# A Fourier-mixing and gated feed-forward kernel: a new order of start-up, weight conversions through PSUM, and the first chunk's outputs in row tiles

## The chip, the cores and the metric

The kernel runs on one core of one Trainium2 chip. Its time is that of one execution on the device in microseconds; the number for a kernel is the median of several executions. One further execution was recorded by the hardware profiler, and every row of the profile comes from that one. TensorE is called PE in the rows (PEld is its weight load), VectorE DVE, ScalarE ACT, GpSimd POOL, and SP is the engine that issues most transfers.

## The reference

The input x has 8 sequences of 3008 rows of 256 numbers. The real part of a two-dimensional Fourier transform of each sequence goes through a gated feed-forward layer of width 1536. Only x is float32; the three weights arrive as float64.

```
X = np.fft.fft(x, axis=1)
X = np.fft.fft(X, axis=2)
h = X.real.astype(np.float32).reshape(8 * 3008, 256)
gate = 1.0 / (1.0 + np.exp(-(h @ w_gate)))
val = h @ w_val
out = (gate * val @ w_out).astype(np.float32)
```

## The kernel before

**The mathematics as tiled.** The transform over the 256 features is a 256x256 cosine/sine matrix (`dt`), and it is multiplied into `w_gate` and `w_val` once, at the start (`merge`, line 329): each of the 2x6 pieces of 256 columns costs four matmuls and gives a piece of `G1` (the cosine half) and `G2` (the sine half). The transform over the 3008 rows is a matmul of folded x against a table of cosines and sines (`ST`, from `stab`): for each sequence it gives two arrays, `pk` and `qk` (`PQE[b][0]` and `PQE[b][1]`), of 128 x 1505. One feature, the middle one of 256, stands apart: its row over the frequencies is `ek`, and its part in the layer is the product of `ek` with a column `ge` taken from the first row of `G2`. The rows and their mirror images share this work: one front tile gives both, as a sum and a difference.

**The loops.** A sequence has 6 chunks of at most 252 frequencies (`chunks`), a chunk 12 tiles of 128 of the 1536 hidden units (`NFT`), so the main loop (line 915 on) has 576 iterations `i`. An iteration does, in program order on each engine:

- `seed` (593), from the second chunk on: ACT writes `ek` times `ge` into a PSUM bank `PF[i]`, once for gate and once for value; `front_a` (602) adds two matmuls with `pk`. In the first chunk there is no seed. For i < 5 (`N1`) two more matmuls, of `G2` with a tile that is zero but for one row of `ek`, do its work; from 5 to 11 DVE does it in `part` (line 619).
- `part` (611) copies twice the bank to SBUF (`ae`); `front_b` (623) adds two matmuls with `qk`. Now the bank holds one of the two row sets, and `ae` minus the bank the other.
- `gate_a` and `gate_b` (628, 647), for tile i-1: sigmoid on ACT, difference and two products on DVE; they give `h`. After the second and third of three tiles POOL forms 13 sums and differences of thirds of `h` (`H_SUMS`, line 660), which the next step needs.
- `back` (667), for the group of three tiles whose first is i-5, i-6 or i-7: a bilinear scheme that multiplies 3x3 blocks of `h` by 3x2 blocks of `w_out` in 15 matmuls of 168 columns, five to an iteration, into five PSUM banks (`po`). It needs sums of `w_out` blocks (`wf`, made by `forms`, 342; POOL makes the first of four groups, DVE the other three). After four groups ACT and DVE copy the banks to `c`, and `finish` (739) sums and transposes them on DVE, a few operations per iteration (`later`), and stores rows. The last group of the program goes another way (`rows_out`, 705): plain `h` as the stationary operand, `w_out` with 256 columns as the moving one.

PSUM has eight banks: five `po` and three that `bank()` hands out in turn.

**The weights.** A piece of 256x256 float64 values is loaded as integers and becomes float32 on three engines: two ACT operations (`weight_parts`, lines 297 and 298), three DVE operations in place in SBUF (`weight_join`, 307, 308, 310), one POOL addition (312). `jobs` gives the order of the 18 pieces, with gate, value and output pieces mixed; the first ten have homes in buffers that are free at the start, the rest use the buffer of x.

**The order of the start (lines 800 to 853)**, which is written out by hand as every engine's order is. SP issues: two weight pieces, x of sequence 0 in two halves, the cosine table in two halves, three pieces, half the sine table, two pieces, the other half, three pieces. The first two pieces are converted and merged; their `ge` columns go from `G2` to `ge` by small transfers on the ACT queue (later ones on SP). x is folded in two halves (`fold_ops(0, 3)`, DVE and a part on POOL), PE makes `pk` and `ek` (the latter with one column of x repeated 128 times as the stationary operand, so that all 128 rows get it), then `qk`. Between the copies of these results six more pieces are converted. Merges 3 to 12 are spread over iterations -1 to 8 (`use`), conversions too (`pre`). Further steps that the change moves: x of sequence 1 is loaded at iteration 14 (`load_x(1)`), and the row of `ek` for the next chunk is fetched eight iterations ahead (`e_rows`).

The helpers `e_load`, `e_fold` and `e_sums` (531 to 567) make the `ek` rows of sequences 1 to 7 later, with seven rows at once and four results at partitions 0, 32, 64 and 96 of one bank.

Of the kernel before, what the change touches and what calls it, by code (L numbers as in the profile page):

```python
# [82 lines left out]
def kernel(  # L83
# [61 lines left out]
    def load_x(b):  # L145
        X[b] = xp.tile([P, 4, NQ, D], F32, name="x4", tag="x4")
        for h in range(0, 4, 2):
            if b:
                nc.sync.dma_start(out=X[b][:, h : h + 2], in_=XR[b][:, h : h + 2])
            else:  # L150
                nc.sync.dma_start(out=X[b][0:NP, h : h + 2], in_=xf[b, :, h : h + 2])
# [29 lines left out]
    G1 = const.tile([P, 2, F], F32, name="G1")  # L181
    G2 = const.tile([P, 2, F], F32, name="G2")
# [9 lines left out]
    def load_table(t, nq):  # L192
        for q in range(0, NQ, nq):
            yield nc.sync.dma_start(out=ST[0][0:NP, t, q : q + nq], in_=stab[:, t, q : q + nq])
# [14 lines left out]
    def table_odd():  # L209
# [21 lines left out]
        def tangent():  # L231
# [12 lines left out]
    KEEP = 10  # L244

    def weight_load(j):
# [13 lines left out]
        def home(j):  # L260

            if j in (0, 1, 2, 3, 5):
                if j > 2:
                    ws = some(5, pqp, "qk")[:, (j // 5) * 2 * WC : (j // 5 + 1) * 2 * WC]
                    return sp.tile([P, 4 * WC], F32, name="raw", tag="sf"), ws
                t = hp.tile([P, 6 * WC], F32, name="raw", tag="h")
                return t[:, 0 : 4 * WC], t[:, 4 * WC :]
            if j in (4, 6, 9):
                t = wf[:, {4: 1, 6: 2, 9: 3}[j]].rearrange("p m n -> p (m n)")
                return t[:, 0 : 4 * WC], t[:, 4 * WC : 6 * WC]  # L270
            t = some(10, cp, "c")
            if j == 7:
                raw = pqp.tile([P, 4 * WC], F32, name="raw", tag="pk")
                return raw, t[:, 6 * WC : 8 * WC]
            return t[:, 0 : 4 * WC], t[:, 4 * WC : 6 * WC]
# [3 lines left out]
        else:  # L279
            both = some(24, xp, "x4").rearrange("p (i n) -> p i n", n=2 * WC)  # L280
            r, i = (j - KEEP) % 3 * 2, 6 + (j - KEEP) % 6
            raw, ws = both[:, r : r + 2].rearrange("p a n -> p (a n)"), both[:, i]
# [17 lines left out]
    def weight_join(j):  # L300
# [4 lines left out]
        wi = ws.bitcast(I32)  # L305
        ts = nc.vector.tensor_scalar
        ts(out=ws, in0=ws, scalar1=2.0 ** -15, scalar2=HUGE, op0=ALU.max, op1=ALU.min)
        ts(out=wi, in0=wi, scalar1=3, scalar2=0x3FFFFFF8, op0=ALU.logical_shift_left,
           op1=ALU.bitwise_and)
        nc.vector.scalar_tensor_tensor(out=wi, in0=hi, scalar=-(2 ** 30), in1=wi,  # L310
# [17 lines left out]

    def merge(ws, g, c, other):
        cs = slice(c * WC, (c + 1) * WC)  # L330
        ps = bank("ps", other)
# [4 lines left out]
        nc.scalar.copy(G2[:, g, cs], ps[:, WC : 2 * WC])  # L336
        nc.scalar.copy(G1[:, g, cs], ps[:, 0:WC])
        for f in range(c * WC // P, (c + 1) * WC // P):
            (nc.sync if c else nc.scalar).dma_start(
                out=ge[:, g, f : f + 1], in_=G2[0:1, g, f * P : (f + 1) * P])  # L340

    def forms(g):
# [4 lines left out]
        engine = nc.vector if g else nc.gpsimd  # L347
# [38 lines left out]
    def fold_ops(b, nq):  # L386
# [51 lines left out]
        else:  # L438

            def half1(q):  # L440
                point(nc.vector, 2, 3, q)
                first(nc.vector, 2, 3, q)
                for blk in range(2):
                    across(nc.vector, blk, q)
                    feat(nc.vector, *parts[blk], q)

            def half2(q):
                across(nc.vector, 0, q)
                feat(nc.vector, *parts[0], q)
                across(pool, 1, q)  # L450
# [545 lines left out]
```

## Time and profile before

| what | value |
|---|---|
| median of 3 runs | 1947.07 us (1945.73 to 1947.19) |
| the profiled execution | 1951.1 us, of which the span of its instructions is 1949.0 us |
| mean granted TensorE clock | 0.997 |
| DMA traffic | 97.85 MB |

The span is counted from the first to the last instruction on the core; the 2.1 us that the execution takes beyond it lie around it. In a timeline row stand the start and the duration in us, the engine, the line, the operation, its output and inputs, the number of instructions, and in brackets the idle time before and what ended it. Two records of PE belong to one float32 matmul of the program, so `x4` of `pf` rows is two matmuls. Matmuls are pipelined: the pace of a series is the difference of the starts of two rows, not the duration of one. In rows of groups stand count, total busy us, mean ns, and idle time before them with its causes. Rows of windows give the busy time and number of instructions per engine in a stretch, then the granted clock, the share of time that the DMA engines were busy, and GB/s.

### The profile page before, as it was taken

The page shows a single profiled execution, that of the slowest core. Times are in us where ns is not written, and L with a number is a line of the kernel's source. Part 1 is how long each engine was busy: PE and PEld are TensorE (multiplying, and loading weights), DVE is VectorE, ACT ScalarE, POOL GpSimd, SP SyncE. Part 2 cuts the span into 40 slices and gives each one's busy share as a digit, 9 for nine tenths or more (in the row PEclk, how much of TensorE's full clock was granted, in tenths as well). Part 3 has the DMA queues.
Part 4 walks back from the last instruction along what each step waited for, and adds up shares of the span by engine and source line. Part 5 has one row for each costly group of instructions (what it writes and reads, how often), then busy time and mean ns, then how long its engine had stood idle before and what let it go on. Part 6 is the DMA issues. An engine that isn't in the chain of part 4 may idle for free.

```text
span 1949.0 us, 34556 instructions
## 1 busy us (share of the span) xinstructions
PE 1917.7 (98%) x11262; PEld 1789.8 (92%) x11262; DVE 1461.0 (75%) x3269; ACT 1332.5 (68%) x3125; POOL 1589.7 (82%) x2842
## 2 busy tenths in 40 slices
PE   6999999999999999999999999999999999999999
PEld 3789889999999999999999999999999999999998
DVE  6777787787777777777777777777777777776776
ACT  3567757776777677776777767777677776777775
POOL 3779998997889878987889878888788886777775
PEclk8999999999999999999999999999999999999999
DMA  8352513212012120222012021221210110011101
GB/s 270 90 145 20 118 32 111 47 25 82 14 47 58 17 79 14 57 49 79 14 25 78 18 79 23 45 53 20 82 20 14 19 23 14 14 20 22 25 16 31
DMA packets 168565, 97.85 MB, mean 50 GB/s; under 512 B 131803, under 2 KB 160070, under 8 KB 165838
## 3 DMA queue, kind: packets, MB, share of 16 engines
q1 hardware_dynamic: 167254, 95.12, 20.5%
q8 instruction: 91, 1.49, 0.3%
q14 instruction: 88, 0.72, 0.1%
q10 hardware_dynamic: 1100, 0.51, 0.1%
q0 software_dynamic: 32, 0.00, 0.0%
HBM read 70.35 MB, written 47.24 MB: 60 GB/s over the span
## 4 chain that ended last, share of the span: by engine, by line
PE 92%; DVE 4%; DMA 2%; ACT 1%; issue 0%; SPq 0%; ACTq 0%; DVEq 0%
PE pf L135 48%; PE po L135 40%; PE ev L135 3%; DMA st<-in_stab_dram 1%; DVE c L754 1%; PE od L135 1%; DMA ge<-G 1%; PE ps L135 1%; DVE z L640 1%; ACT pf L653 0%; DVE h L654 0%; DVE h L652 0%; PE row L135 0%; DVE wf L375 0%; DMA raw<-in_moe_w_val_dram 0%
## 5 line engine op out<-in xcount | busy, mean ns | idle before, releaser
L660 POOL TENSOR_TENSOR sf<-h 128x168 f32<-128x168 f32 (+1 forms) x955 | 530.8, 574 | 225.1 <-DVE h L654 225.0
L660 POOL TENSOR_TENSOR sf<-h,sf 128x168 f32<-128x168 f32 (+1 forms) x1146 | 638.4, 576 | 61.5 <-DVE h L654 60.9
L135 PE MATMUL pf<-qk,G 128*128 128x252 f32 (+1 forms) x2304 | 583.2, 376 | 4.2 <-DVE ae L619 2.3
L135 PE MATMUL pf<-pk,G 128*128 128x252 f32 (+1 forms) x2304 | 583.5, 376 | 1.6 <-DVE h L654 1.4
L654 DVE TENSOR_TENSOR h<-pf,z 128x252 f32<-128x252 f32 (+1 forms) x576 | 241.5, 419 | 420.0 <-ACT pf L653 420.0
L600 ACT ACTIVATE pf<-ek,ge 128x252 f32<-128x252 f32 (+1 forms) x1128 | 531.4, 471 | 18.7 <-DVE h L654 0.2
L135 PE MATMUL po<-sf,wf 128*128 128x168 f32 (+1 forms) x3056 | 527.5, 305 | 0.0
L616 ACT ACTIVATE ae<-pf 128x504 f32<-128x504 f32 (+1 forms) x569 | 335.0, 589 | 233.8 <-PE pf L135 232.5
L135 PEld LDWEIGHTS pf<-pk,G 128*128 128x128 f32 x2304 | 436.1, 190 | 55.7 <-DVE h L654 3.2
L135 PEld LDWEIGHTS po<-sf,wf 128*128 128x128 f32 x3056 | 470.4, 190 | 8.2
L135 PE MATMUL po<-h,wf 128*128 128x168 f32 (+1 forms) x2674 | 473.9, 306 | 0.2 <-DVE wf L372 0.2
L754 DVE TENSOR_TENSOR c<-c 128x168 f32<-128x168 f32 (+1 forms) x949 | 450.6, 506 | 5.2
L135 PEld LDWEIGHTS po<-h,wf 128*128 128x128 f32 x2674 | 425.5, 190 | 17.2 <-DVE wf L372 0.6
L135 PEld LDWEIGHTS pf<-qk,G 128*128 128x128 f32 x2304 | 409.9, 190 | 31.6 <-ACT ae L616 3.1
L640 DVE TENSOR_TENSOR z<-ae,pf 128x504 f32<-128x504 f32 (+1 forms) x569 | 378.4, 665 | 25.0 <-ACT h L635 23.4
L635 ACT ACTIVATE h<-pf 128x252 f32<-128x252 f32 (+1 forms) x576 | 217.7, 378 | 155.5 <-PE pf L135 147.8
L653 ACT ACTIVATE pf<-z 128x252 f32<-128x252 f32 (+1 forms) x576 | 214.4, 372 | 113.7 <-DVE h L652 111.1
L652 DVE TENSOR_TENSOR h<-h,pf 128x252 f32<-128x252 f32 (+1 forms) x576 | 232.3, 403 | 0.0
L660 POOL TENSOR_TENSOR sf<-sf 128x168 f32<-128x168 f32 (+1 forms) x191 | 109.5, 573 | 15.0
L660 POOL TENSOR_TENSOR sf<-sf,h 128x168 f32<-128x168 f32 (+1 forms) x191 | 104.2, 545 | 0.0
L135 PE MATMUL ev<-st,x 63*128 63x189 f32 (+3 forms) x372 | 73.1, 347 | 9.4 <-DVE x L403 6.6
L688 ACT COPY c<-po 128x504 f32<-128x504 f32 (+1 forms) x144 | 81.7, 568 | 0.0
(148 smaller groups left out, 888.8 us busy)
## 6 DMA issues: line engine op xcount, KB each, us to landing
x<-xr SPq DMA_DIRECT2D x14, 1536.0 KB
out_dram<-os SPq DMA_DIRECT2D x376, 56.0 KB
xr<-in_xf_dram SPq DMA_DIRECT2D x14, 768.0 KB
xr<-in_xf_dram SPq DMA_DIRECT2D x35, 256.0 KB
ek<-ed SPq DMA_DIRECT2D x39, 126.0 KB
out_dram<-os SPq DMA_DIRECT2D x288, 7.0 KB
st<-in_stab_dram SPq DMA_DIRECT2D x4, 1111.9 KB
x<-in_xf_dram SPq DMA_DIRECT2D x2, 1512.0 KB
```

Of the source, the lines that this page charges most:

```text
L135: nc.tensor.matmul(o, l, r, start=start, stop=stop, skip_group_check=True)
L600: nc.scalar.activation(PF[i][:, g], EK[i // NFT], AF.Copy, scale=ge[:, g, f : f + 1])
L616: nc.scalar.activation(AP[i], PF[i], AF.Copy, scale=2.0)
L635: nc.scalar.activation(H[p][:, fh, 0:n], PF[i][:, 0], AF.Sigmoid)
L640: nc.vector.tensor_tensor(z[:, :, ::-1], AP.pop(i), PF[i], op=ALU.subtract)
L652: nc.vector.tensor_tensor(h[:, fh, 0:n], h[:, fh, 0:n], pf[:, 1], op=ALU.mult)
L653: nc.scalar.activation(pf[:, 0], z[:, 0], AF.Sigmoid)
L654: nc.vector.tensor_tensor(h[:, fh, n:], pf[:, 0], z[:, 1], op=ALU.mult)
L660: nc.gpsimd.tensor_tensor(block(p, dst), block(p, a), block(p, b), op=(ALU.subtract, ALU.add)[op])
L688: (nc.vector.tensor_copy if t == 1 or t == 3 and not last else nc.scalar.copy)(C[0][:, 3 * t * R : 3 * (t + 1) * R], PO[t][:, 0 : 3 * R])
L754: engine.tensor_tensor(t[:, dst * R : (dst + 1) * R], *v, op=(ALU.subtract, ALU.add)[op])
```

## The change

- **Order of loads.** Eight weight pieces first, then x of sequence 0 in three slices of two of six table rows each (128 partitions instead of 126), each followed by its slice of the cosine table (split into 112 and 14 partitions), then the sine table in three slices, then six more pieces; the last four after x is used up. `jobs` puts the twelve gate and value pieces ahead of the six output pieces.
- **Start.** Fourteen matmuls on a tile of ones (`warm`), then eight pieces converted and merged in a row. x is folded in thirds, all on DVE. The `ek` row of sequence 0 is now made as a single row with four results at partitions 0, 32, 64 and 96 of a bank (`e0_sums`), then copied, combined (`e0_copies`, `e0_row`) and spread over the partitions by one matmul with a row of ones (`e0_spread`). Between the three parts of the `qk` sums stand the first three `front_a`.
- **Conversions.** The first two DVE operations of `weight_join` write to a PSUM bank, the third reads from there.
- **`ge`.** One matmul of one column per tile, of `G2`'s first row with a one, and one copy (`ge_sums`), in place of transfers.
- **Chunk 0's tiles.** All have seeds, so the extra matmuls for i < 5 and the DVE path for 5 to 11 go. The join of a weight stands between the two DVE products of `gate_b`. `merge` has one ACT copy of 512 columns in place of two of 256. Merges 9 to 12 stand in iterations 0 to 3.
- **Chunk 0's outputs.** No `H_SUMS` and no bilinear products for the first four groups; instead `rows_start`: per tile four matmuls with `h` as the stationary operand and a 256-column row block of `w_out` as the moving one, into two banks; at the end four copies and four stores, and no `finish`.
- All `forms` on POOL; `load_x(1)` at iteration 18; `e_rows` eleven iterations ahead.

```diff
+    def load_third(j):
+        q = slice(2 * j, 2 * j + 2)
+        rows = xf.rearrange("b p h q d -> (b p) h q d")
+        nc.sync.dma_start(out=X[0][:, :, q], in_=rows[0:P, :, q])
-    jobs = [(0, 0), (1, 0), (0, 1), (1, 1), (2, 0), (0, 2), (1, 2), (2, 1), (0, 3), (1, 3), (0, 4), (2, 2),
-            (1, 4), (0, 5), (1, 5), (2, 3), (2, 4), (2, 5)]
+    jobs = [(w, c) for c in range(NPR) for w in range(2)] + [(2, c) for c in range(NPR)]
...
+        mid_ = ws if other is None else bank("join", other).rearrange("p (c f) -> p c f", c=2)
+        mi = mid_.bitcast(I32)
-        ts(out=ws, in0=ws, scalar1=2.0 ** -15, scalar2=HUGE, op0=ALU.max, op1=ALU.min)
-        ts(out=wi, in0=wi, scalar1=3, scalar2=0x3FFFFFF8, op0=ALU.logical_shift_left,
+        ts(out=mid_, in0=ws, scalar1=2.0 ** -15, scalar2=HUGE, op0=ALU.max, op1=ALU.min)
+        ts(out=mi, in0=mi, scalar1=3, scalar2=0x3FFFFFF8, op0=ALU.logical_shift_left,
            op1=ALU.bitwise_and)
-        nc.vector.scalar_tensor_tensor(out=wi, in0=hi, scalar=-(2 ** 30), in1=wi,
+        nc.vector.scalar_tensor_tensor(out=wi, in0=hi, scalar=-(2 ** 30), in1=mi,
                                        op0=ALU.bitwise_and, op1=ALU.bitwise_or)
...
-        for f in range(c * WC // P, (c + 1) * WC // P):
-            (nc.sync if c else nc.scalar).dma_start(
-                out=ge[:, g, f : f + 1], in_=G2[0:1, g, f * P : (f + 1) * P])
+    def merged(j):
+        g, c = jobs[j]
+        ps = MERGED.pop((g, c))
+        cs = slice(c * WC, (c + 1) * WC)
+        nc.scalar.copy(G[:, :, g, cs], ps.rearrange("p (h n) -> p h n", h=2))
+    def ge_sums(js, other=None):
+        ps = bank("ge", other)
+        at_ = [(jobs[j][0], f) for j in js for f in range(2 * jobs[j][1], 2 * jobs[j][1] + 2)]
+        for g, f in at_:
+            mm(ps[:, g * NFT + f : g * NFT + f + 1], G2[0:1, g, f * P : (f + 1) * P], busy[0:1, 0:1],
+               True, True)
...
-        engine = nc.vector if g else nc.gpsimd
+        engine = nc.gpsimd
...
+            def third(q):
+                a, m = x4[:, 0:3:2, q], x4[:, 1:4:2, q]
+                tt(a[:, :, :, 0], a[:, :, :, 0], m[:, :, :, 0], op=ALU.add)
+                tt(a[:, :, :, 1:D], a[:, :, :, 1:D], m[:, :, :, D - 1 : 0 : -1], op=ALU.add)
+                across(nc.vector, 0, q)
+                across(nc.vector, 1, q)
+            def feats(q):
+                v, r = x4[:, 0:2, q], x4[:, 2:4, q]
+                nc.vector.memset(r[:, :, :, 0:1], 0.0)
+                lo, hi = v[:, :, :, 1:HD], v[:, :, :, D - 1 : HD : -1]
+                tt(r[:, :, :, 1:HD], lo, hi, op=ALU.subtract)
+                tt(lo, lo, hi, op=ALU.add)
...
+    def e0_sums(j):
+        if not j:
+            E0["ps"] = bank("pe", NB - 1)
+        for q in (2 * j, 2 * j + 1):
+            for blk in range(2):
+                c0, n = ((0, NE), (NE, NO))[blk]
+                row = (2 * blk + q % 2) * TB
+                mm(E0["ps"][row : row + 1, 0:n], W[0, blk][2][:, q], ST[0][0:NP, 0, q, c0 : c0 + n],
+                   not j, j == N3 - 1)
+    def e0_copies():
...
+        for i in range(4):
+            nc.scalar.copy(a[i], ps[i * TB : i * TB + 1, 0 : a[i].shape[1]])
+    def e0_row():
...
+        places(er, 0, True, od, ev)
+        places(er, 1, False, ev1, od1)
+    def e0_spread():
+        ps = bank("ek", NB - 1)[:, 0:CH]
+        mm(ps, busy[0:1, 0:P], shared["er"][:, 0:CH], True, True)
+        EK[0] = ekp.tile([P, CH], F32, name="ek", tag="ek")
+        nc.scalar.copy(EK[0], ps)
...
-    def gate_b(i):
+    def gate_b(i, between=()):
         nc.vector.tensor_tensor(h[:, fh, 0:n], h[:, fh, 0:n], pf[:, 1], op=ALU.mult)
         nc.scalar.activation(pf[:, 0], z[:, 0], AF.Sigmoid)
+        for f in between:
+            f()
         nc.vector.tensor_tensor(h[:, fh, n:], pf[:, 0], z[:, 1], op=ALU.mult)
-        if p == len(groups) - 1:
+        if p < NG or p == len(groups) - 1:
             return
...
+    def rows_start(p, part):
+        f = 3 * p + part
+        n = chunks[0][1]
+        tiles = [(0, P), (P, n - P), (n, P), (n + P, n - 1 - P)]
+        if not f:
+            PO[:] = [pso.tile([P, 2 * WC], F32, name="rows", tag=f"po{NB - 2 + i}") for i in range(2)]
+        ps = [PO[i // 2][0:rows, i % 2 * D : (i % 2 + 1) * D] for i, (_, rows) in enumerate(tiles)]
+        for i, (r0, rows) in enumerate(tiles):
+            mm(ps[i], H[p][:, part, r0 : r0 + rows], WO[f // 2][:, f % 2], not f and i % 2 == 0,
+               f == NFT - 1)
...
+    load_x(0)
+    for j in range(8):
+        weight_load(j)
+    for j in range(N3):
+        load_third(j)
+        load_table(0, j)
+    warm(14)
+    for j in range(8):
+        weight_parts(j)
+        if j > 2:
+            merged(j - 3)
+        weight_join(j, j % NB)
+        weight_use(j)
+    for j in range(5, 8):
+        merged(j)
+    ge_sums(range(8), 3)
+    for j in range(N3):
+        load_table(1, j)
+    for j in range(8, KEEP):
+        weight_load(j)
...
+    for j in range(N3):
+        folds[2 * j]()
+        e0_sums(j)
+        folds[2 * j + 1]()
+        if j == N3 - 1:
+            e0_copies()
+            e0_row()
+        for sums, _, _ in cos:
+            sums(2 * j, 2 * j + 1)
+    put = [then() for _, then, _ in cos]
+    for f in put:
+        f()
+    e0_spread()
+    for i in range(N3):
+        seed(i)
+    for j in (8, 9):
+        weight_parts(j)
+        weight_join(j, NB - 1)
...
+    sines(0)
+    first(0)
+    sines(1)
+    first(1)
+    sines(2)
+    first(2)
+    for _, then, _ in sin:
+        then()()
+    for j in range(KEEP, len(jobs)):
+        weight_load(j)
+    nc.sync.dma_start(out=ed[0:1], in_=shared["er"])
+    weight_parts(10)
...
+    for j, i in ((8, -2), (9, -1), (10, 0), (11, 1), (12, 2), (13, 4), (14, 6), (15, 8), (16, 10), (17, 12)):
+        if i > 0:
+            pre.setdefault(i - 1, []).append(lambda j=j: weight_parts(j))
+        if i >= 0:
+            mid.setdefault(i, []).append(lambda j=j: weight_join(j, 2))
+        use.setdefault(i + 2, []).append(lambda j=j: using(j))
+        if jobs[j][0] < 2:
+            use.setdefault(i + 3, []).append(lambda j=j: ge_sums((j,), (j + 1) % 2))
```

More of the change, by code (lines that the diff above doesn't have):

```diff
@@ L795, in finish @@
         add(lambda: (flip(1, 0), store(1)))
+    busy = ekp.tile([P, CH], F32, name="busy", tag="ek")
+    nc.vector.memset(busy, 1.0)
     nc.gpsimd.memset(nil, 0.0)
@@ L854, with warm @@
-    weight_use(2)
+    for j in range(N3):
+        load_third(j)
+        load_table(0, j)
+    def warm(n):
+        ps = bank("warm", NB - 1)
+        for _ in range(n):
+            mm(ps[:, 0:CH], busy[:, 0:P], busy, True, True)
+    shared["er"] = pqp.tile([P, NK + 1], F32, name="er", tag="pk")[0:1]
+    warm(14)
[7 more added lines that the diff above has]
+        merged(j)
@@ new lines, with sines, first @@
+    for f in put:
[6 more added lines that the diff above has]
+        weight_join(j, NB - 1)
+    sin = [seq_group(0, blk, 1, (2 * blk, 2 * blk + 1)) for blk in range(2)]
+    def sines(j):
+        for sums, _, _ in sin:
+            sums(2 * j, 2 * j + 1)
+    def first(i):
+        front_a(i)
+        if i < 2:
+            part(i)
+    sines(0)
[6 more added lines that the diff above has]
+        then()()
```

204 lines of the change are left out of this document (77 added, 127 removed).

## The prediction

> **What bounds the kernel now.** I read the page first, then windows cut where the start changes its nature.
>
> ```profile
> PE 1917.7 (98%) x11262; PEld 1789.8 (92%) x11262; DVE 1461.0 (75%) x3269; ACT 1332.5 (68%) x3125; POOL 1589.7 (82%) x2842
> ...
> 0.00:21.96 21.96, 6.70 (x16) 5.09 (x16) 10.40 (x19) 5.22 (x10) 6.81 (x11) 0.91 0.86 302
> 21.96:56.27 34.31, 31.53 (x97) 19.77 (x98) 26.10 (x45) 13.49 (x25) 14.62 (x12) 0.91 0.80 225
> 56.27:127.98 71.71, 65.32 (x333) 56.78 (x332) 56.56 (x112) 39.65 (x106) 53.54 (x81) 1.00 0.33 99
> 127.98:177.98 50.00, 50.00 (x289) 47.12 (x288) 37.22 (x85) 35.74 (x84) 43.16 (x75) 1.00 0.49 78
> ```
>
> PE is the bound everywhere but in the first 128 us: from 127.98 on it has no gap. Only the start can gain, and what it gains reaches the end one for one, because a later start of the same back-to-back stream is all that is moved. So the question is when `front_b(16)`, the first of the last window's steady tiles, ends. The timeline of PE gives the marks.
>
> ```profile
> 8.70 6.70 PE L135 MATMUL ps<-raw,dt 128*128 128x256 f32 x16 [8.70 <-POOL raw L312]
> 21.96 2.88 PE L135 MATMUL ev<-st,x 126*128 126x377 f32 x4 [6.56 <-DVE x L403]
> ...
> 45.48 1.63 PE L135 MATMUL ev<-st,x 126*128 126x377 f32 x2 [2.78 <-DMA st<-in_stab_dram]
> ...
> 51.06 1.89 PE L135 MATMUL ps<-raw,dt 128*128 128x256 f32 x8
> 52.79 1.01 PE L135 MATMUL pf<-pk,G 128*128 128x252 f32 x4
> ...
> 56.27 1.01 PE L135 MATMUL pf<-qk,G 128*128 128x252 f32 x4
> ...
> 127.13 1.01 PE L135 MATMUL pf<-qk,G 128*128 128x252 f32 x4
> 127.98 1.01 PE L135 MATMUL pf<-pk,G 128*128 128x252 f32 x4
> 128.83 1.59 PE L135 MATMUL po<-h,wf 128*128 128x168 f32 x10
> 130.26 1.01 PE L135 MATMUL pf<-qk,G 128*128 128x252 f32 x4
> ```
>
> Paces, from starts: two matmuls of 252 columns 0.85 us (127.98 to 128.83), five of 168 columns 1.43, so 1.69 ns a column; a steady tile 3.13 (127.13 to 130.26); a merge 1.73 (51.06 to 52.79); 377 columns 0.64. The first 16 records took 6.70 us, twice the 3.46 of two later merges: PE begins slow. `front_b(0)` starts at 56.27 and `front_b(16)` ends at 127.98, 71.7 us later. The work between is 17 `front_b` and 16 `front_a` (28.1), eight merges (13.8), the extra products of tiles 1 to 4 (3.4) and 12 `back` parts (17.1): 62.4, so 9.3 us are stalls. The groups of DVE in this window name their cause.
>
> ```profile
> L310 DVE SCALAR_TENSOR_TENSOR wx<-wx 128x512 int32<-128x512 int32 x8 | 7.6, 949 | 0.3
> L654 DVE TENSOR_TENSOR h<-pf,z 128x252 f32<-128x252 f32 x16 | 6.7, 420 | 9.7 <-ACT pf L653 9.7
> ...
> L307 DVE TENSOR_SCALAR wx<-wx 128x512 f32<-128x512 f32 x8 | 4.7, 590 | 0.0
> L308 DVE TENSOR_SCALAR wx<-wx 128x512 int32<-128x512 int32 x8 | 4.7, 582 | 0.3
> ```
>
> DVE is busy 56.6 of 71.7 us and idles 9.7 of the rest behind ACT's sigmoid: in this stretch DVE's chain sets the pace, with joins of 2.12 us (949 + 590 + 582 ns) and `forms` between gates.
>
> **The change, step 1: the marks before the loop.** What the joins, folds and transfers cost:
>
> ```profile
> 4.90 0.66 ACT L297 ACTIVATE raw<-raw 128x512 f32<-128x512 f32 x1 [2.67 <-DMA raw<-in_moe_w_gate_dram]
> ```
>
> ```profile
> 5.59 0.43 DVE L307 TENSOR_SCALAR raw<-raw 128x512 f32<-128x512 f32 x1 [5.59 <-ACT raw L297]
> 6.05 0.43 DVE L308 TENSOR_SCALAR raw<-raw 128x512 int32<-128x512 int32 x1
> 6.52 0.69 DVE L310 SCALAR_TENSOR_TENSOR raw<-raw 128x512 int32<-128x512 int32 x1
> ```
>
> ```profile
> 7.36 1.28 POOL L312 TENSOR_TENSOR raw<-raw 128x512 int32<-128x512 int32 x1 [5.24 <-DVE raw L310]
> ```
>
> ```profile
> L406 DVE TENSOR_TENSOR x<-x 126x768 f32<-126x768 f32 x3 | 2.9, 953 | 0.0
> ...
> L504 ACT COPY a<-ev 128x377 f32<-128x377 f32 x3 | 1.4, 470 | 3.0 <-PE ev L135 3.0
> ...
> L688 DVE COPY c<-po 128x504 f32<-128x504 f32 x1 | 0.7, 672 | 0.0
> ...
> L509 DVE TENSOR_TENSOR pk<-a,od 128x376 f32<-128x376 f32 x1 | 0.5, 539 | 0.0
> ```
>
> ```profile
> 0.00:10.00 10.00, 1.30 (x3) 1.13 (x4) 3.58 (x6) 3.92 (x6) 2.56 (x7) 1.00 0.77 274
> 10.00:20.00 10.00, 5.40 (x14) 3.96 (x13) 4.91 (x10) 1.29 (x4) 4.25 (x4) 0.91 0.95 327
> 20.00:30.00 10.00, 8.04 (x21) 4.80 (x22) 9.74 (x15) 2.49 (x4) 4.44 (x4) 0.75 1.00 311
> 30.00:40.00 10.00, 10.00 (x33) 5.94 (x32) 7.41 (x14) 3.68 (x7) 3.93 (x3) 1.00 1.00 242
> ```
>
> *Transfers.* The rates add up to 2.74, 6.01, 9.12 and 11.54 MB at 10, 20, 30 and 40 us. I take the same curve. The eight pieces (0.52 MB each, with `dt` 4.45) are in at 15; the third slice of x (9.12 MB) at 30.0, of the cosines at 33, of the sines (12.15) at 43.7, pieces 8 to 11 at some 45.5 to 50.7.
>
> *Joins.* Alone and in SBUF a join takes 1.53 us (5.59 to 7.12 by the pace), beside POOL 2.12. Through PSUM no row shows it; the nearest is the copy from PSUM, 0.67 for 504 columns, which gives 0.70 + 0.70 + 0.61 = 2.0 where each waits for the one before. Bounds 1.5 and 2.2; I take 2.0, by that row. The Trainium skill speaks against this edit: "VectorE: DVE Perf Modes", section "Why PSUM operands drop a tier", says that an operand in PSUM takes fp32 work of one source from two elements a cycle to one; 0.43 against 0.67 us agrees; by the rule a join is the 2.0 taken, without it 1.5, and the eight would end 3.8 earlier. From 5.6, eight joins end at 21.6 (bounds 17.8 and 23.2); ACT (1.2 a piece) and the transfers keep up. POOL's addition 1.3, the merge 1.73 and its copy bring `ge_sums` to 25.4. `warm`, 14 matmuls from about 1 us, lies under the wait of 8.70 and costs at most a late first merge, which catches up at 1.73 against 2.0.
>
> *ge.* Sixteen matmuls of one column, 32 records:
>
> ```profile
> L135 PEld LDWEIGHTS po<-sf,wf 128*128 128x128 f32 x3056 | 470.4, 190 | 8.2
> ```
>
> ```profile
> L135 PEld LDWEIGHTS pe<-st,x x24: 89/91/99, 203.2 to 204.6; 126*7 126x7 f32 x24
> ```
>
> ```profile
> 203.28 2.13 PE pe L135 x24
> ```
>
> A record can't cost less than a load: 0.09 to 0.19 us, 2.9 to 6.1 in all; I take 0.15, 4.8 us, to 30.2. The Trainium skill ("TensorE: Matmul & The Clock Gate", section "LDWEIGHTS (loading the stationary operand)") gives columns/1.2 ns, by which 32 would be an estimated 3.4 us and the sum 1.4 less.
>
> *Folds and sums.* A third has 3060 elements a partition, at 953/768 ns 3.8, with small ones 4.1 us, all on DVE: 21.6 to 25.8, to 30.0, to 34.1. The single-row `ek` sums are like the `pe` rows, four at a time: 12 matmuls in 2.13 us, in place of 7.6 for the 12 matmuls of 377 columns that `ek` takes now (those alone would be a gain of 5.5). So PE needs 0.7 + 2.54 (four matmuls of 377) a third: from 30.2 to 39.9, always behind DVE. Then the row: four ACT copies (470 ns) and four DVE operations (539) after the third `e0_sums` at 37.4 reach 41.0; PE waits 1.1 us for `e0_spread`. `pk` is complete at 42.9. Three sine thirds and three `front_a`, 3 x (2.54 + 0.85), run from 41.4 to 51.6; the sines are in at 43.7, before the third. The merge of piece 8 ends at 53.3, and the four DVE operations of `qk` end there too, behind joins 8 and 9 (pieces in at 47, joins done by 50.6). So `front_b(0)` starts at 53.3 instead of 56.27, with three `front_a` done.
>
> **Step 2: the loop to `front_b(16)`.**
>
> ```profile
> 1937.07 5.34 PE L135 MATMUL row<-tail,h 128*128 128x256 f32 x24
> ...
> 1942.25 1.93 PE L135 MATMUL row<-tail,c 128*128 128x128 f32 x16
> ```
>
> `rows_start` is what the last group does today: 24 records from 1937.07 to 1942.25, 0.216 each, so a tile's four matmuls cost 1.73, 0.30 more than the 1.43 of the bilinear products; over 12 tiles **+3.6 us** of PE. The sum: 17 `front_b` 14.4, 14 `front_a` (tiles 3 to 16) 11.9, merges 9 to 11 5.2, four `ge_sums` of two matmuls 2.4, 12 row tiles 20.7: 54.6 us against 62.4 of work and 71.7 of time. The first-five products (3.4) are gone, five merges moved ahead.
>
> What feeds it: DVE loses the `forms`, its ge path and, after chunk 0, `finish`; per tile it keeps 1.3 and eight joins of 2.0: 38 of 55 us. ACT spent 35.7 us on 16 steady tiles (2.2 a tile); 17 tiles, seven conversions of 1.2 and the small copies make 50 of 55, near enough for some stalls. POOL:
>
> ```profile
> L660 POOL TENSOR_TENSOR sf<-h 128x168 f32<-128x168 f32 (+1 forms) x955 | 530.8, 574 | 225.1 <-DVE h L654 225.0
> ```
>
> ```profile
> L372 POOL TENSOR_TENSOR wf<-wf 128x256 f32<-128x256 f32 (+1 forms) x4 | 2.8, 710 | 0.1
> ```
>
> four groups of 13 sums at 574 ns go (30 us), three groups of `forms` come (some eight operations at 0.71, 17 us). The last two groups of them meet the first sums of chunk 1 in iterations 14 to 18, where POOL falls some 6 us behind; the products use the sums three iterations (9.4 us) later, so nothing waits. SP issues fewer transfers: no `ge`, four stores for chunk 0; `e_rows(12)`, now at iteration 1, holds SP until the last `ge_sums` (iteration 4) frees its buffer, with nothing behind it before the copies of x at 9; `load_x(1)` at 18 leaves over 20 us before the first fold of it at iteration 25. I set 2 us for stalls (bounds 0 and 9, today's value). `front_b(16)` ends at 53.3 + 54.6 + 2 = 109.9, **18 us earlier** than 127.98. Where chunk 0's `finish` goes off DVE nothing is gained, PE having no gap there.
>
> **The sum.** The profiled execution took 1951.1 us, 1949.0 of it the span; it becomes 1933.1, and the median of 1947.07, which lies 4.0 lower, 1929.
>
> **Rivals.**
> (a) *Cheaper than I took.* Joins at 1.53, `ge` at 2.9, no stalls: then the third x slice at 30.0 binds, DVE ends at 34.1, PE at 36.7 instead of 39.9. Gain 3.2 + 2 = 5 more, 1924.
> (b) *Transfers bind.* x stands behind 4.2 MB of weights. At the 242 GB/s of the fourth window from 10 us on, the third slice lands at 36.4, the cosine sums end at 43, piece 9 lands at 53, its join ends at 56.6 (on ACT and DVE the copies and sums of `qk` stand behind it), `qk` at 59: 6 us lost, 1935. For: the sine wait of 2.78 us at 45.48 today, DMA shares of 1.00. Against: pieces 8 to 13 no longer mix with the tables, and 128 rows replace 126.
> (c) *The loop stays at DVE's and ACT's pace*, with today's 9 us of stalls or so: 1937. For: ACT at 50 of 55 us, in order, with conversions ahead of sigmoids. Against: the DVE work that made today's stalls is gone.
> (d) *Slower.* The join stands between the two products of `gate_b`, so it lengthens the time that a tile holds one of three PSUM banks. If the eight joins of 2.1 (17 us) and the seven conversions of 1.2 ahead of the next sigmoid (8) all come upon PE, 25 us are lost, and the kernel takes 1954. It is slower from the point where over 18 of these 25 are bare. Against: DVE idles 9.7 us in just this place today, and the bank is needed only an iteration later.
> (e) *It moves the loss only*: PE waits in the loop what it saved before it; 1947.
>
> **How the numbers follow.** Forecast 0.46, (a) 0.12, (b) 0.15, (c) 0.16, (d) 0.07, (e) 0.04. The likeliest is 1929, with 1925 to 1933 as its own range. The range takes in (a) and (c) with room for (b) at 200 GB/s: 1921 to 1942. A measurement of this kernel can't tell a change under 0.2% (3.9 us) from none. Faster 0.89, the same 0.04, slower 0.07.
>
> **What would show it.** Step 1: `pf<-qk` begins at 51 to 56 us; joins show 0.6 to 0.7 us with PSUM outputs; the `pe`-like sums overlap. Step 2: row-tile records at a pace of 0.216; steady tiles of 3.13 us from about 110 us, 18 before today's. Wrong: a wait of PE over 3 us on x, sines or a weight (b), idle PE behind ACT or `h` in 53 to 110 (c, d), or POOL's sums making PE wait near 115 to 130.

## The result, and the profile after

| | before | after |
|---|---|---|
| median, measured together on one chip | 1947.13 us (10 runs, 1945.39 to 1954.70) | 1943.20 us (10 runs, 1941.72 to 1946.44) |
| ratio after / before, 95% interval | | 0.9978 [0.9968, 0.9989] |
| the profiled execution | 1951.1 us, span 1949.0 | 1941.99 us, span 1940.2 |

The kernel became faster, but by 4 us and not by 18: 1943.2 lies outside the predicted range of 1921 to 1942. The gain is 0.2%, just the size that the prediction gives as the least that can be told from none; the interval of the ratio lies below 1. Three windows of the changed kernel come first; the cuts are the end of the eighth merge, the start of `front_b(0)`, the first tile without a weight merge, and the end of `front_b(16)`. The columns are those of the windows of before.

```profile
26.36:54.80 28.44, 28.44 (x128) 17.60 (x128) 19.76 (x37) 13.29 (x27) 2.60 (x2) 0.94 0.94 262
54.80:80.49 25.69, 18.51 (x81) 14.98 (x80) 13.03 (x25) 13.75 (x34) 5.14 (x4) 0.93 0.25 83
80.49:119.04 38.55, 38.55 (x182) 34.05 (x181) 23.48 (x47) 31.46 (x82) 24.07 (x39) 1.00 0.33 96
```

PE has no gap from 26.36 to 54.80 and none from 80.49 to 119.04. Between them it idles 7.18 of 25.69 us. The timeline of PE shows the marks of the forecast and the place of the idle time.

```profile
26.36 3.73 PE L135 MATMUL ge<-busy,G 1*128 1x1 f32 x32
30.02 1.11 PE L135 MATMUL pe<-st,x 126*1 126x377 f32 x8
31.05 1.63 PE L135 MATMUL ev<-st,x 126*128 126x377 f32 x2
...
35.13 0.81 PE L135 MATMUL pe<-st,x 126*1 126x377 f32 x8
...
38.60 0.81 PE L135 MATMUL pe<-st,x 126*1 126x377 f32 x8
...
42.07 0.69 PE L135 MATMUL ek<-er,busy 1*128 1x252 f32 x2
...
54.80 1.01 PE L135 MATMUL pf<-qk,G 128*128 128x252 f32 x4
55.74 0.60 PE L135 MATMUL ge<-busy,G 1*128 1x1 f32 x4
59.21 1.96 PE L135 MATMUL ps<-raw,dt 128*128 128x256 f32 x8 [2.87 <-ACT ge L360]
...
64.13 3.37 PE L135 MATMUL ps<-wc,dt 128*128 128x256 f32 x8 [1.58 <-ACT ge L360]
...
72.60 1.96 PE L135 MATMUL ps<-wc,dt 128*128 128x256 f32 x8 [2.58 <-ACT ge L360]
...
78.77 1.89 PE L135 MATMUL rows<-wc,h 128*128 128x256 f32 x8
80.49 1.01 PE L135 MATMUL pf<-qk,G 128*128 128x252 f32 x4
...
83.92 1.01 PE L135 MATMUL pf<-qk,G 128*128 128x252 f32 x4
...
118.19 1.01 PE L135 MATMUL pf<-qk,G 128*128 128x252 f32 x4
119.04 1.01 PE L135 MATMUL pf<-pk,G 128*128 128x252 f32 x4
```

`front_b(0)` starts at 54.80 (forecast 53.3). `front_b(16)` ends at 119.04 (forecast 109.9). Three merges, of pieces 9, 10 and 11 (counted from 0, as the code counts them), wait for ACT's copy of `ge`, 7.03 us in all, and one of them then takes 3.37 us instead of 1.96. The view of waits gives PE's sum over the whole span:

```profile
PE ps L135 <- ACT ge L360: 7.0, 3, 2.9
```

The code says why a merge waits for a copy of `ge`. In the loop `ge_sums((j,), (j + 1) % 2)` writes its two columns into the bank that `weight_use(j + 1, (j + 1) % 2)` takes next, right behind it in the same iteration. The merge of piece j + 1 can't start before the columns have been read from that bank. ACT's timeline shows when it gets to reading them:

```profile
57.03 0.59 ACT L664 ACTIVATE ae<-pf 128x504 f32<-128x504 f32 x1 [0.75 <-DVE z L679]
57.52 0.38 ACT L692 ACTIVATE pf<-z 128x252 f32<-128x252 f32 x1
57.82 0.65 ACT L301 ACTIVATE wc<-wc 128x512 f32<-128x512 f32 x1
58.37 0.65 ACT L302 ACTIVATE wc<-wc 128x512 int32<-128x512 uint32 x1
58.91 0.15 ACT L360 COPY ge<-ge 128x2 f32<-128x2 f32 x1
```

PE's `ge` products end at 56.34 (55.74 + 0.60). Ahead of the copy of 0.15 us stand `part`'s copy, which waits 0.75 us for a DVE operation, a sigmoid, and the two conversions of a later weight. So the theory to test was: **the shared bank costs this 7 to 9 us.** The other part of the miss had to be in the sum, since 1929 lies 1819.1 below the forecast mark of 109.9 (1929 − 109.9), while the profiled execution took 1823.0 us beyond its own (1941.99 − 119.04).

### The profile page after: what moved, and what is told of

It reads as the page before. It is cut to its first block, busy times and chain, and to the rows that moved or that the text cites. A ratio compares the mean times of both kernels' runs of the same rounds, so it can differ in the third digit from the quotient of the medians.

```text
span 1940.2 us, 34490 instructions
## 1 busy us (share of the span) xinstructions
PE 1923.7 (99%) x11296; PEld 1793.6 (92%) x11296; DVE 1432.2 (74%) x3210; ACT 1347.6 (69%) x3151; POOL 1563.8 (81%) x2806
## 4 chain that ended last, share of the span: by engine, by line
PE 95%; DVE 3%; ACT 1%; issue 0%; DMA 0%; POOL 0%; ACTq 0%; DVEq 0%
PE pf L135 49%; PE po L135 40%; PE ev L135 3%; PE rows L135 1%; PE od L135 1%; DVE c L819 1%; PE ps L135 1%; DVE z L679 0%; ACT pf L692 0%; PE row L135 0%; DVE join L314 0%; DVE h L691 0%; DVE h L695 0%; PE pe L135 0%; DVE join L313 0%
## 5 line engine op out<-in xcount | busy, mean ns | idle before, releaser
L701 POOL TENSOR_TENSOR sf<-h 128x168 f32<-128x168 f32 (+1 forms) x935 | 517.9, 573 | 213.1 <-DVE h L695 213.1
L701 POOL TENSOR_TENSOR sf<-h,sf 128x168 f32<-128x168 f32 (+1 forms) x1122 | 625.0, 577 | 58.1 <-DVE h L695 57.8
L653 ACT ACTIVATE pf<-ek,ge 128x252 f32<-128x252 f32 (+1 forms) x1152 | 542.7, 471 | 18.9
L135 PE MATMUL po<-sf,wf 128*128 128x168 f32 (+1 forms) x2992 | 516.1, 305 | 0.0
L135 PEld LDWEIGHTS po<-sf,wf 128*128 128x128 f32 x2992 | 460.6, 190 | 8.1
L135 PE MATMUL po<-h,wf 128*128 128x168 f32 (+1 forms) x2618 | 463.2, 305 | 0.0
L819 DVE TENSOR_TENSOR c<-c 128x168 f32<-128x168 f32 (+1 forms) x929 | 437.9, 503 | 5.1
L135 PEld LDWEIGHTS po<-h,wf 128*128 128x128 f32 x2618 | 416.5, 190 | 16.2
L679 DVE TENSOR_TENSOR z<-ae,pf 128x504 f32<-128x504 f32 (+1 forms) x576 | 383.4, 666 | 42.1 <-ACT h L678 40.5
L828 DVE STREAM_TRANSPOSE os<-c 128x256 f32<-128x256 f32 x184 | 70.7, 422 | 0.3 <-issue 0.3
```

Source lines behind the costliest of these rows:

```text
L135: nc.tensor.matmul(o, l, r, start=start, stop=stop, skip_group_check=True)
L653: nc.scalar.activation(PF[i][:, g], EK[i // NFT], AF.Copy, scale=ge[:, g, f : f + 1])
L679: nc.vector.tensor_tensor(z[:, :, ::-1], AP.pop(i), PF[i], op=ALU.subtract)
L701: nc.gpsimd.tensor_tensor(block(p, dst), block(p, a), block(p, b), op=(ALU.subtract, ALU.add)[op])
L819: engine.tensor_tensor(t[:, dst * R : (dst + 1) * R], *v, op=(ALU.subtract, ALU.add)[op])
L828: nc.vector.transpose(os_[0][:, s, 0:nb, h, :], t[:, c0 : c0 + nb * TB])
```

## The experiments

The four profiled executions of before and the seven of changed kernels, by two marks: the start of `front_b(0)` and the end of `front_b(16)` (starts of PE's `pf<-qk` rows, the second with the 0.85 us of two matmuls added). The names are those of the runs described below. `b_again`, `a_gebank`, `a_order` and `a_joinsb` ran on one chip, `b_third` and `b_fourth` on a second, the last three on a third; each ratio is to the kernel before on the same chip.

```
kernel      front_b(0)  front_b(16)  time of that   time less
             starts       ends        execution    second mark
before        56.27      127.98       1951.10        1823.1
b_again       53.01      123.43       1946.12        1822.7
b_third       55.10      126.55       1949.66        1823.1
b_fourth      53.39      124.85       1947.69        1822.8
after         54.80      119.04       1941.99        1823.0
a_order       54.92      119.96       1942.80        1822.8
a_joinsb      57.54      121.78       1944.52        1822.7
a_gebank      54.69      110.67       1933.45        1822.8
g_nowarm      55.11      111.10       1933.97        1822.9
a_gemix       52.70      109.51       1932.49        1823.0
a_gemix9      52.01      109.26       1932.21        1823.0
```

The last column is the same within 0.4 us in all eleven. So the time of an execution is read off its second mark: it is that mark and 1822.9, and what differs between these executions lies ahead of it. A mark says where in an execution time was lost; it is still one execution of each kernel.

**Before once more** (`b_again`, `b_third`, `b_fourth`). The kernel before was profiled three more times, unchanged.

> The kernel before, unchanged, profiled once more. Its first profiled execution took 1951.1 us, 4.0 above the median of its runs, while the changed kernel's profiled one lies 1.2 below its median; so 8.8 us of span stand against 3.9 us of medians. Theory: the first profile of before drew a slower start (granted clock 0.997), and this one shows a span near 1945 us with the end of front_b(16) near 124 us instead of 127.98, and the rest of the span equal to 1821.0 us within 0.5. Rival: the start is the same each time (127.98) and it is the part after it that varies, by 4 us.

> The kernel before, unchanged, a third profiled execution. If the late start of the first one (first product with qk at 56.27 us, after a wait of 2.78 for the sine table) is a rare draw, this one looks like the second: front_b(0) at 53 +- 0.5, front_b(16) ending at 123.4 +- 1, a time near 1946. Rival: the wait on the sine table comes about every second time; then front_b(0) stands at 55 to 57, and the median of the kernel before holds part of it.

> The same kernel once more, with the same two expectations: 53 +- 0.5 and 123.4 +- 1 if the late start is rare, 55 to 57 if it comes about every second time.

The first sine sum in the timeline of PE, in `b_again` and then in `b_third`:

```profile
43.36 0.80 PE L135 MATMUL ev<-st,x 126*128 126x377 f32 x2
```

```profile
44.48 0.90 PE L135 MATMUL ev<-st,x 126*128 126x377 f32 x2 [0.21 <-DMA st<-in_stab_dram]
```

The wait for the sine table, 2.78 us in the first profile, is 0.21 us in `b_third` and absent in the other two. `b_again` is as its theory had it: its mark is 123.43, and its span beyond the mark 1820.9 us. The expectations of the last two were too neat: `b_third` fits the rival at its start, without the wait that the rival names, and `b_fourth` lies between. What holds is that the start of the kernel before varies over these four executions by 4.5 us (123.43 to 127.98; the two on one chip differ by 1.7), and the first profile was the latest of four. Its median of 1947.1 belongs to a mark of 124.2 (1947.1 − 1822.9).

**The bank of `ge`** (`a_gebank`). Only the bank of the columns changes: 3 and 4 in turn for pieces 8 to 10, and 0 for piece 11.

```diff
-            use.setdefault(i + 3, []).append(lambda j=j: ge_sums((j,), (j + 1) % 2))
+            use.setdefault(i + 3, []).append(lambda j=j: ge_sums((j,), 3 + j % 2 if j < 11 else 0))
```

> The changed kernel, with the bank of ge_sums for pieces 8 to 10 no longer the one into which the next merge goes (banks 3 and 4, and 0 for piece 11, after the last merge). Theory (same bank): PE's waits of 2.87, 1.58 and 2.58 us on the ge copy at 59.21, 64.13 and 72.60 go, with the slow merge of 3.37 us behind the second; front_b(16) ends 6 to 8.5 us earlier than 119.04, time 1935 to 1937, 6 to 8 below the changed kernel. Rival (ACT is the bound in iterations 0 to 4): the same time is lost in waits on ACT's seeds, sigmoids or copies of merges, and under 3 us are won.

Measured: 1933.62 us (1932.26 to 1935.10), ratio to before 0.9936 [0.9922, 0.9949]. The same stretch of PE's timeline in this kernel:

```profile
54.69 1.01 PE L135 MATMUL pf<-qk,G 128*128 128x252 f32 x4
55.63 0.60 PE L135 MATMUL ge<-busy,G 1*128 1x1 f32 x4
56.16 1.99 PE L135 MATMUL ps<-raw,dt 128*128 128x256 f32 x8
...
59.51 0.60 PE L135 MATMUL ge<-busy,G 1*128 1x1 f32 x4 [0.51 <-ACT G L349]
...
110.67 1.01 PE L135 MATMUL pf<-pk,G 128*128 128x252 f32 x4
```

The merge now follows the `ge` products at once. `front_b(0)` starts where it did (0.11 us earlier), and `front_b(16)` ends 8.4 us earlier: the 7.03 of waits without the 0.51 that is left, the 1.41 of the slow merge (3.37 less 1.96), and 0.3 that I don't place. By the two ratios to before it is 8.2 us (0.9978 less 0.9936, of 1947). The mark moved as the theory had it, and the time came out 1.4 us under its 1935 to 1937. The bank is the cause. A window of the same stretch, whose idle time is 0.65 us:

```profile
54.69:110.67 55.98, 55.33 (x262) 47.84 (x261) 36.52 (x72) 44.85 (x115) 29.19 (x43) 1.00 0.34 104
```

**The order on ACT** (`a_order`). The rival within this theory: the bank does no harm if the copy stands ahead of the conversions.

```diff
-        todo = pre.pop(i, []) + use.pop(i, [])
+        todo = use.pop(i, []) + pre.pop(i, [])
```

> The changed kernel with one reordering: in an iteration the merge and ge_sums (with their ACT copies) come before weight_parts of a later piece, banks as they are. Theory (same bank, the copy standing behind 1.2 us of weight_parts on ACT): each of the first and third waits gets 1.1 us shorter, the second, which has no weight_parts in front, stays; 2 to 4 us won, 1939 to 1941. Rival (ACT is the bound): the work that is only put in another order wins nothing, 1943.

Measured: 1944.06 us (1939.21 to 1947.20), ratio to before 0.9990 [0.9981, 0.9999]: nothing won over the changed kernel, where 2 to 4 us were expected. Its three merges that wait, and its ACT queue, by the timelines of PE and ACT:

```profile
58.94 3.61 PE L135 MATMUL ps<-raw,dt 128*128 128x256 f32 x8 [2.47 <-ACT ge L360]
...
66.23 3.38 PE L135 MATMUL ps<-wc,dt 128*128 128x256 f32 x8 [2.30 <-ACT ge L360]
...
73.34 1.96 PE L135 MATMUL ps<-wc,dt 128*128 128x256 f32 x8 [1.50 <-ACT ge L360]
```

```profile
55.60 0.67 ACT L301 ACTIVATE wc<-wc 128x512 f32<-128x512 f32 x1
...
56.73 0.36 ACT L678 ACTIVATE h<-pf 128x252 f32<-128x252 f32 x1
...
58.63 0.17 ACT L360 COPY ge<-ge 128x2 f32<-128x2 f32 x1
```

At the first two places the conversions are ahead of the copy all the same: those of the iteration before now stand in front of this iteration's sigmoids, and push these back. The first copy comes 0.28 us earlier (58.63 for 58.91). Only the third wait gets shorter as the theory had it (1.50 for 2.58); the second grows (2.30 for 1.58). All three together are 6.27 us for 7.03, and that is more than given back, since two merges instead of one run slow. The order within an iteration doesn't help; the dependency has to go.

**Conversions in SBUF** (`a_joinsb`). The change sends the first two operations of a join through PSUM. Taken back:

```diff
-        mid_ = ws if other is None else bank("join", other).rearrange("p (c f) -> p c f", c=2)
+        mid_ = ws
```

> The changed kernel with the joins in place in SBUF again. By the row of before a join alone takes 1.53 us and beside POOL 2.12; through PSUM the changed kernel shows 2.06 to 2.2 a join. Theory: SBUF joins take 1.5 to 1.9 in the start, DVE ends the eight 2 to 4 us earlier, but PE, which follows at 2.0 a merge and then has the ge and cosine sums to do without a gap, ends them only 1 to 3 us earlier; time 1940 to 1943. Rival: DVE and POOL share a path in SBUF, joins grow to over 2.1 and POOL's additions over 1.5 us, and the time rises to 1944 to 1948.

Measured: 1947.40 us (1944.47 to 1948.99), ratio to before 1.0004 [0.9995, 1.0013], slower than the changed kernel by 4.2 us in the medians (5.1 by the two ratios to before) and 2.7 at the second mark. The theory missed; of the rival, the time and the longer joins came, while POOL's additions stayed at 1.35 us. The second operation of a join among DVE's groups between 5.3 and 22.2 us, in the changed kernel:

```profile
L314 DVE TENSOR_SCALAR join<-join 128x512 int32<-128x512 int32 x8 | 5.6, 699 | 0.3
```

In SBUF it takes 0.43 us alone, as in the first join, and 1.40 beside POOL's addition. DVE's and POOL's timelines of `a_joinsb`:

```profile
5.81 0.43 DVE L314 TENSOR_SCALAR raw<-raw 128x512 int32<-128x512 int32 x1
...
10.25 1.40 DVE L314 TENSOR_SCALAR raw<-raw 128x512 int32<-128x512 int32 x1
```

```profile
10.01 1.35 POOL L318 TENSOR_TENSOR raw<-raw 128x512 int32<-128x512 int32 x1 [1.60 <-DVE raw L316]
```

It ends at 11.65, 0.29 us after POOL's addition ends at 11.36, so most of it was waiting out that addition; six of the eight joins have such an operation of 1.39 to 1.40 us. Through PSUM each operation costs 0.69 to 0.70 us, POOL or not, and a join 2.06 us; in SBUF it is 2.48 (0.43 and 1.40 for the two operations in place of twice 0.70), and the eighth merge starts at 27.23 instead of 24.43. The rule weighed in the prediction ("VectorE: DVE Perf Modes", section "Why PSUM operands drop a tier", in the Trainium skill) holds, with 0.69 against 0.43 us; it is outweighed by another one, in "SBUF — State Buffer", section "SBUF: two separate sides", also in the Trainium skill: VectorE and GpSimd share one pair of ports, and whoever has it holds it for the whole instruction. The two rows above agree with that.

**Without `warm`** (`g_nowarm`). The kernel of `a_gebank` less one line.

```diff
-    warm(14)
```

> a_gebank (1933.6 us) without the fourteen matmuls on ones at the start. Theory: PE's first matmuls run at half pace until it has been busy for a few us (in the kernel before 16 records took 5.8 to 6.7 us instead of 3.5), here on merges 0 to 2, which then take 3.4 us against the joins' pace of 2.06; PE falls 2.5 to 4 us behind and wins back 0.33 a merge, so the end of merge 7 comes 0 to 2 us later, time 1933.5 to 1936. Rival: with PE waiting between merges the half pace goes on through all eight, the end of merge 7 comes 6 us or more later, time 1938 to 1941.

Measured: 1933.97 us (1933.82 to 1934.63), ratio to before 0.9933 [0.9921, 0.9946], against 0.9936 with `warm` on another chip. PE's first merges here, and then in `a_gebank`:

```profile
9.01 7.56 PE L135 MATMUL ps<-raw,dt 128*128 128x256 f32 x24 [9.01 <-POOL raw L318]
...
24.76 1.99 PE L135 MATMUL ps<-wf,dt 128*128 128x256 f32 x8 [1.00 <-POOL wf L318]
```

```profile
9.81 5.34 PE L135 MATMUL ps<-raw,dt 128*128 128x256 f32 x24
...
24.33 1.99 PE L135 MATMUL ps<-wf,dt 128*128 128x256 f32 x8 [1.01 <-POOL wf L318]
```

Without `warm` the first three merges take 2.2 us longer, start 0.8 earlier and have caught up all but 0.43 us at the eighth. That is as the theory had it. The second marks of the two executions differ by 0.4 us as well (111.10 and 110.67), less than executions of one kernel scatter, so the runs can't tell whether `warm` is worth anything.

**`ge` spread out** (`a_gemix`). On top of `a_gebank`, the columns of the first eight pieces stand behind each merge's copy, all in one bank kept for them, instead of 32 records in a row. `ge_mm` is the matmuls of `ge_sums`, `ge_copy` its copy.

```diff
+    ge_bank = bank("ge", 3)
...
-        weight_join(j, j % NB)
+        weight_join(j, (0, 1, 2, 4)[j % 4])
         weight_use(j)
+        if j > 2:
+            ge_mm(ge_bank, (j - 3,))
     for j in range(5, 8):
         merged(j)
-    ge_sums(range(8), 3)
+        ge_mm(ge_bank, (j,))
+    ge_copy(ge_bank, range(8))
```

> a_gebank with the ge matmuls of the first eight pieces put one piece at a time behind the merges (each behind the merge three pieces later), one copy at the end, and the joins in four banks. PE has 0.33 us free in each 2.06 us of a join, and after the merges only three pieces (1.4 us) are left of the 3.7 us stretch. Theory: 2 us are won there, and 1 to 2 more because the cosine sums behind it no longer run at half pace (3.1 us for four records at 30.93 to 33.6 in a_gebank); front_b(0) comes 1 to 3 us earlier and is then held by the join of piece 9 and the four qk operations of DVE; time 1930.5 to 1932.5. Rival: the ge matmuls delay the merges, and nothing is won (1933 to 1935).

Measured: 1931.95 us (1931.40 to 1932.82), ratio to before 0.9923 [0.9910, 0.9935]: the time of the theory, and the lowest median of all here. Its interval overlaps that of `a_gebank`, which ran on another chip, so the runs don't settle the gain over that one; all five runs lie below the five of `g_nowarm` on the same chip (1933.82 to 1934.63). A window of the changed kernel shows what is gained, the first cosine sums behind the run of one-column products:

```profile
31.05:33.73 2.68, 2.68 (x8) 1.51 (x5) 2.06 (x4) 0.00 (x0) 0.00 (x0) 0.50 1.04 232
```

Two sums of 377 columns (the four records from 31.05 on) take 2.68 us there at a granted clock of 0.50. In `a_gemix` the same two take 1.37 (29.59 to 30.96), at a granted clock of 1.00:

```profile
29.59 0.90 PE L135 MATMUL ev<-st,x 126*128 126x377 f32 x2
...
30.96 0.79 PE L135 MATMUL ev<-st,x 126*128 126x376 f32 x2
...
39.26 0.69 PE L135 MATMUL ek<-er,busy 1*128 1x252 f32 x2
...
52.70 1.12 PE L135 MATMUL pf<-qk,G 128*128 128x252 f32 x4 [0.26 <-DVE qk L535]
...
58.35 0.60 PE L135 MATMUL ge<-busy,G 1*128 1x1 f32 x4 [1.23 <-ACT G L349]
```

`e0_spread` comes 2.8 us earlier than in the changed kernel (39.26 against 42.07); part of it is given back to waits for `qk` and ACT, and against `a_gebank` 1.7 us are left by the medians, 1.2 by the second marks of one execution each.

**Piece 9 later** (`a_gemix9`). On top of `a_gemix`, the conversion of piece 9 moves behind the operations that make `qk`.

```diff
-    for j in (8, 9):
-        weight_parts(j)
-        weight_join(j, NB - 1)
+    weight_parts(8)
+    weight_join(8, NB - 1)
...
+    weight_parts(9)
+    weight_join(9, NB - 1)
     weight_parts(10)
```

> a_gemix with the conversion of piece 9 put behind the four DVE operations that finish qk, its merge staying in iteration 1. Theory: those operations wait behind the join of piece 9 (its transfer lands at 47.9 us) once PE comes earlier; 0.5 to 2 us under a_gemix, 1929.5 to 1931.5. Rival: the late join holds up its merge in iteration 1 by as much, no gain.

Measured: 1932.47 us (1932.21 to 1933.10), ratio to before 0.9926 [0.9912, 0.9939]. PE's timeline:

```profile
54.38 1.99 PE L135 MATMUL ps<-raw,dt 128*128 128x256 f32 x8 [0.40 <-POOL raw L318]
...
58.10 0.60 PE L135 MATMUL ge<-busy,G 1*128 1x1 f32 x4 [0.88 <-ACT G L349]
```

`front_b(0)` starts 0.7 us earlier, and the time is gone in the wait for piece 9's addition and for ACT. Nothing is won, as the rival had it.

## Why the prediction was wrong

The forecast of 1929 is 14.2 us below the median of 1943.2. By its own steps: `front_b(0)` 1.5 us late (54.80 for 53.3), the loop 7.6 us longer (64.2 for 56.6), the sum 3.9 us off (1823.0 for 1819.1 beyond the mark), and the median 1.2 above the profiled execution. That makes 14.2.

- **The failing step is "I set 2 us for stalls (bounds 0 and 9, today's value)".** The feeders were costed as rates (DVE 38, ACT 50 of 55 us), but not the one hard dependency that the new lines bring: `ge_sums` and the next merge in one bank, with a copy between them that stands in ACT's queue behind sigmoids and, at two of three places, behind the conversions of a weight. In place of 2 us it cost 7.03 of waits (7.18 with all idle time of PE) and 1.41 in a slow merge. The idle time lies within the bounds of 0 and 9, but these were taken from stalls of another cause. Without the next error, of 3.9 us, the measured time would have come within the range. It was to be read from the diff: the argument `(j + 1) % 2` and the `j % 2` of the next piece are the same bank. The Trainium skill ("PSUM — Partial Sum Buffer", section "PSUM bank collisions raise a hardware error") has the rule that would have called for it: a compiler's scheduler adds a dependency between any two instructions on different engines that touch the same 32 partitions of one bank. The trace agrees, with 1.58 to 2.87 us at three such places. The work of 54.6 us itself was nearly right: in `a_gebank` the loop takes 55.98, with 0.65 idle, where 56.6 was forecast. Today's value of 9.3 us was read too high as idle time: the prediction's own window has PE busy for 65.32 of 71.71 us, so 6.39 idle.
- **The sum's "which lies 4.0 lower" was the second error.** Those 4 us between the profiled execution of before and the median lay in the stretch that the change replaces, in a start that was late in this execution. They were already in the 18 us gain, and were taken a second time. Against the typical mark of 124.2 the forecast of 109.9 is worth 14.3 us, that is 1932.8. That is close to what a kernel without the bank wait shows: 1933.6. The prediction's "from 127.98 on it has no gap" holds for its window, to 177.98. Beyond the mark PE idles 6.8 us in all, most of it in the last 49 us, and as long in the changed kernel, so this didn't enter the difference.
- **The marks before the loop.** Joins were forecast at 2.0 and take 2.06; the eight end at 21.95 for 21.6, where DVE's timeline of the changed kernel goes on to x:

```profile
21.95 0.16 DVE L464 TENSOR_TENSOR x<-x 126x4 f32<-126x4 f32 x1
...
31.80 0.17 DVE L464 TENSOR_TENSOR x<-x 126x4 f32<-126x4 f32 x1 [0.59 <-DMA x<-in_xf_dram]
```

`ge_sums` was forecast to end at 30.2 and does at 30.02: 3.7 us for 32 records instead of 4.8, begun 1.0 us later. That the mark agrees is luck, two errors that cancel. The estimate of 3.4 by the Trainium skill ("TensorE: Matmul & The Clock Gate", section "LDWEIGHTS (loading the stationary operand)") was nearer. Not foreseen was the half pace of the first cosine sums (1.3 us), and a third takes 3.47 us on PE where 3.24 was forecast. So the cosine sums end at 42.07 for 39.9, and at `e0_spread` PE waits for nothing, where 1.1 us for `er` were forecast.
- **Row tiles.** The records run at the 0.216 us that was forecast (78.77 to 80.49, eight in 1.72), and a tile takes 3.43 us (80.49 to 83.92). Neither the first sums of chunk 1 nor `e_rows` or `load_x(1)` makes PE wait; steady tiles begin at 119.04.
- **The rivals.** (a) fell: joins take their 2.06 us. (b) has no row: x lands late (its third slice at 31.80 for 30.0), and DVE idles 0.59 us for it, but PE waits on no transfer. (c) names an idle PE behind ACT, which came, but by one dependency and not by ACT's rate: with the bank changed ACT keeps up with 44.9 busy us of 55.98. (d) and its price of 25 us did not come: with the join still between the gate products, PE idles 0.65 us in the whole loop of `a_gebank`. (e) comes closest in time (1947), and is right in kind: of the 12.5 us that `a_gebank` gains on before (1946.11 on its chip), 8.4 are lost again in the changed kernel to a wait in the loop.

What stays open in part is why the median of the changed kernel lies 1.2 us above its profiled execution, and that of `a_joinsb` 2.9. Each run has its mean granted clock on record, and the two go together: in the changed kernel 0.998 at 1941.7 and 1942.0 us (the latter is the profiled one), 0.997 at 1943.1 to 1943.2, 0.996 at 1944.5 to 1944.7 and 0.995 at 1946.4; in `a_joinsb` from 0.998 at 1944.5 to 0.995 at 1948.7 to 1949.0. So the longer executions had more time at a lower clock, as a further slow merge of 1.41 us would give. Which stage it was no profile shows.

## What to carry to other kernels

When a diff puts a small product and a large one into the same PSUM bank in turn, the copy between them is a barrier for PE, as long as everything that stands ahead of that copy on its engine: read the bank arguments of neighbours before adding up rates. A profiled execution that is slower than the median is to be placed before it is subtracted: if its excess lies in the stretch that the change replaces, it must not be carried over as an offset. A mark late in the start, beyond which all executions took the same time within 0.4 us, shows in which stage an execution lost its time; it doesn't take away the scatter of the start itself, which was 4.5 us over four executions of the kernel before.

## What the runs showed of the hardware

- A DVE operation with one source, in SBUF, waits out a POOL addition of two SBUF operands (1.40 for 0.43 us); through PSUM it doesn't (0.70, with POOL or without).
- PE's clock was granted at half with no idle time in the 5.6 us ahead, behind a run of narrow products: 0.50 in the 2.68 us from 31.05 on, where 32 one-column records had run from 26.36 to 30.02, and 1.00 at the same place in `a_gemix`, where the records are spread over the merges. A wait of 1.01 us that the eighth merge had at 24.43 is gone there too, so that the narrow products alone do it is argued, not shown. In the loop it was 1.00 in the merge behind a pause of 2.87 us and 0.56 in the merge behind one of 1.58, as two windows of the changed kernel show.

```profile
59.21:61.01 1.80, 1.80 (x9) 1.59 (x9) 0.50 (x2) 0.00 (x0) 1.29 (x1) 1.00 0.17 64
...
64.13:67.29 3.16, 3.16 (x9) 2.52 (x9) 1.71 (x3) 0.00 (x0) 1.28 (x1) 0.56 0.02 5
```

The Trainium skill ("TensorE: Matmul & The Clock Gate", section "What's actually happening") has the clock halve after an idle window of about 3.4 us and says that the window runs free of the instructions. The half pace agrees; the idle time doesn't, since 1.58 us were enough once and 2.87 weren't, so here the length of a pause alone doesn't tell what the next matmul costs. How long the half pace lasted is the same at both places, if the clock is taken as either full or half: 3.4 us by the windows and their neighbours (0.68 in the 1.03 us from 30.02, 0.50 in 2.68, 0.97 in the 1.40 behind; 0.56 in 3.16, 0.72 in the 1.18 behind).
